# An attention and two-MoE kernel whose first part is issued on each engine in program order

## The chip, the cores and the metric

The kernel runs on one core of a Trainium2 chip. Its engines are TensorE (PE, matmuls, with the weight loads as PEld), VectorE (DVE), ScalarE (ACT), GpSimd (POOL) and SyncE (SP, which here issues DMAs); each works through its own list of instructions in order and waits at semaphores for the others. The metric is the time of one execution on the device in microseconds (us), as a median of several runs.

## What is computed

An attention over a softmax memory, then two gated layers, all in float32:

```python
a = phi - np.max(phi, axis=2, keepdims=True); a = np.exp(a)
a = a / (np.sum(a, axis=2, keepdims=True) + 1e-09)          # softmax over the sequence
k_m = np.einsum('bhsm,bhsd->bhmd', a, k); v_m = np.einsum('bhsm,bhsd->bhmd', a, v)
scores = scale * np.matmul(q, k_m.transpose(0, 1, 3, 2))    # then a softmax over the 32 memories
attn_out = np.matmul(attn, v_m)                             # q, k, v: (4, 8, 576, 64), phi: (4, 8, 576, 32)
# x: (2304, 512), its rows normalized by their root mean square and rms_g
x = (silu(x @ w_gate) * (x @ w_val)) @ w_out                # 512 -> 1536 -> 512
h = x @ w_in; g = where(h >= 1, h, where(h <= -1, 0, (h + 1) ** 2 / 4)); out = g @ w_out2   # 512 -> 2048 -> 512
```

A float32 product is made from three products of a high and a low part (names ending in h and l).

## The kernel before

The program has two parts. P1 computes the attention and the first MoE layer, P2 (L1040 `hp`, L1065 `acc`) the second. P1 is written as many small generator functions, called streams. Each stream yields, before each piece of its work, which engine it needs and for how long ("V", 2.12), or that it takes or gives a buffer, or that it waits for a flag that another stream sets. An `Agenda` object holds all streams with a model of time: engine by engine it keeps when the engine is free, adds a small latency (`HOP`) when work passes from one engine to the next, and always goes on with the stream that can start earliest; at a tie a priority decides. When a stream goes on, its instructions are written into the program. So the program's order is the order of this model. Some steps leave the choice of the engine to the model ("VAhi", "GAlow", "VAsign", "VGlo", "VGal").

Before, this order is not the order of issue: the Tile framework's own scheduler takes the program and orders the instructions of each engine again, by its own estimate. Only instructions named in `tc.keep_in_program_order` keep their place against each other: all loads of phi, k, v and q, the first 24 (`KEEP`) loads of raw weights, and the small `heat` matmuls (L480) that keep TensorE busy early on.

The streams that matter here:
- `loads` issues the loads of phi, k, v and q of the four batches on SP.
- `soft(b)`, one for each batch b: the maximum over the sequence (`pm`, L423, VectorE), its spreading by TensorE (`mps`, L429 and L446), the subtraction from `phi` (L452, VectorE), the exponent (L459, ScalarE), then four sums on GpSimd (`half` and `s`, L466 to L469).
- `memory(b)`: `kvps` (L501, TensorE) sums the exponents with k and v and L514 adds the sums `s`; VectorE divides (`r`, `kd`, `vs`, L524 to L549).
- nine pairs of queries (half a batch each, and one for the rests): `qps`, `sc`, `e`, `aT`, `xp`, `ATp`, `Ah`, `Al`.
- `convert` (L240 on): raw weights arrive as 64-bit words in one of four `raw` buffers; ScalarE, VectorE and GpSimd turn them into float32 (`w`, `cx`: L261, L264, L266, L270, L280, L282), for the output weight of the first layer also into two parts (`wo1h`, `wo1l`, L289, L291). Weights of the gate and value products come first (raw0, raw1 and so on), then the output weight, then P2's weights, which go back to HBM (`w_d`).
- `vwps` (L769) multiplies the weights with the memory's values; `vwh`, `vwl` (L789) are its two parts. `gv` (L818) makes `gps` and `vps` from them in 48 chunks, 12 a batch, in two halves each; `gate` (L846 `th`, L849 `ah`, L851 `al`) forms their product. `out1` (L876) makes `ops` from `ah`, `al` and the output weight; a stream of it first waits for the flag ("wo1", 0), which is set when six units of that weight are converted.

In names like kvps1_0 the first number is the batch, in gps4_1 the chunk and its half, in ops0_0 the batch and the output's part.

Of the kernel before, what the change touches and what calls it, by code (L numbers as in the profile page):

```python
# [25 lines left out]
ORDER = [0, 1, 2, 3, 8, 4, 5, 6, 7]  # L26

BANKS = {"g": (0, 1), "v": (2, 3), "o": (4, 5), "p": (0, 1, 2, 3), "w": (6, 7), "q": (2, 3), "s": (1,), "x": (2, 3), "a": (0,), "t": (5,), "k": (7,), "m": (4,), "l": (4,)}

KEEP = 24  # L30

HEAT = (6, ("A", (0, 0)), 2.09, 0.34)

# [11 lines left out]
class Agenda:  # L45
# [22 lines left out]
    def add(self, pri, stream):  # L68
        self.count += 1
        self._go([pri, self.count, stream, None, self.done, ""], None)  # L70
# [34 lines left out]
    def run(self, stop=None):  # L105
        while self.live and not (stop and stop in self.flags):
            best = None
            for x in self.live:
                s = self._start(x)
                if s is not None:  # L110
                    key = (max(s[0], self.now), x[0], x[1])
                    if best is None or key < best[0]:
                        best = key, x, s[1]
            assert best is not None, [(x[0], x[3]) for x in self.live]
            (at, _, _), x, z = best
            self.live.remove(x)
            self.now = at
            kind, arg = x[3]
            value = None
            done = at  # L120
            if kind == "take":
                self.room[arg] -= 1
            elif kind == "give":
                self.room[arg] += 1
            elif kind == "rest":
                done += arg
            elif kind == "flag":
                x[5] = ""
            elif kind == "heat":
                tick = int(at / TICK)  # L130
                value = self.ticks.get(tick, 0.0) < HEAT[2]
                if value:
                    slow = 1.0 if self.ticks.get(tick - 1, 0.0) > WARM else 2.0
                    self.ticks[tick] = self.ticks.get(tick, 0.0) + arg
                    done = self.free["P"] = at + arg * slow
            else:
                value = kind[z]
                t = arg[z] if isinstance(arg, tuple) else arg
                if value == "P":
                    tick = int(at / TICK)  # L140
                    slow = 1.0 if self.ticks.get(tick - 1, 0.0) > WARM else 2.0
                    self.ticks[tick] = self.ticks.get(tick, 0.0) + t * DUTY.get(kind, 1.0)
                    t *= slow
                done = self.free[value] = at + t
                x[5] = value
            self.done = done
            x[4] = x[4] + 0.5 if kind == "Dq" else done
            self._go(x, value)


def tile_attn_moe(tc, q, k, v, phi, w_gate, w_val, w_out1, rms_g, w_in2, w_out2, out):
# [10 lines left out]
    nc = tc.nc  # L162
    B, H, S, D = q.shape
    M = phi.shape[3]
# [72 lines left out]
    def convert(src, pieces, dst, split, done):  # L237
# [4 lines left out]
        nconv[0] += 1  # L242
        raw = wv.tile([P, CU, 2], U32, tag="raw", name=f"raw{n}", bufs=BUFS["raw"])
        rs = raw.rearrange("p n t -> p (n t)")
        i = nc.sync.dma_start(out=rs.rearrange("p (c f) -> p c f", c=pieces) if pieces > 1 else rs, in_=src)
        if n < KEEP:
            tc.keep_in_program_order(i)
        yield "rest", DMA_LAG
        if split:
            yield "take", "x"  # L250
# [105 lines left out]
    def loads():  # L356

        seq = []
        for b in range(B):
            seq += [("phi", b), ("kv", b)]  # L360
        for i, pr in zip(Q_AT, q_loads, strict=True):
            seq.insert(i, ("q", pr))
        for s in seq:
            yield "take", "qr" if s[0] == "q" and s[1][0] == B else s[0]
            if s[0] == "phi":
                b = s[1]
                yield "Dq", 1.8
                t = phi_t[b] = ld.tile([P, 4, J, M], F32, tag="phi", name=f"phi{b}", bufs=BUFS["phi"])
                tc.keep_in_program_order(
                    nc.sync.dma_start(out=t.rearrange("p c j m -> p c (j m)"), in_=by_half(phi[b], J * M))  # L370
                )
            elif s[0] == "kv":
                b = s[1]
                t = kv_t[b] = ld.tile([P, 2, 4, J, D], F32, tag="kv", name=f"kv{b}", bufs=BUFS["kv"])
                for i, src in ((0, k), (1, v)):
                    yield "Dq", 3.6
                    tc.keep_in_program_order(
                        nc.sync.dma_start(
                            out=t[:, i].rearrange("p c j d -> p c (j d)"), in_=by_half(src[b], J * D)
                        )  # L380
                    )
            else:
                b = s[1][0]
                yield "Dq", 3.4 if b < B else 0.45 * len(per_batch(s[1]))
                if b == B:
                    t = q_t[s[1]] = ld.tile([P, H, LJ, D], F32, tag="qr", name=f"qr{s[1][1]}", bufs=BUFS["qr"])
                    for bb, rows in per_batch(s[1]):
                        tc.keep_in_program_order(
                            nc.sync.dma_start(
                                out=t[rows],  # L390
                                in_=q[bb, :, SM:S, :].rearrange("h (p j) d -> p h j d", j=LJ),
                            )
                        )
                else:
                    t = q_t[s[1]] = ld.tile([P, H, QJ, D], F32, tag="q", name=f"q{b}", bufs=BUFS["q"])
                    tc.keep_in_program_order(
                        nc.sync.dma_start(
                            out=t.rearrange("p h j d -> p h (j d)"),
                            in_=q[b, :, 0:SM, :].rearrange("h (p j) d -> p h (j d)", j=QJ),
                        )  # L400
                    )
            add(0, arrived(s))
        for name in ("phi", "kv", "q", "qr"):
            for _ in range(BUFS[name]):
                yield "take", name
        mark("inputs")

    def by_half(x, n):

        return x.rearrange("h s d -> (h s d)").rearrange("(c q x) -> q c x", c=4, x=n)  # L410
# [62 lines left out]
    def heat():  # L473

        yield "take", ("bank", HEAT[0])
        t = psum.tile([P, 512], F32, tag=f"b{HEAT[0]}", name="heat")
        while HEAT[1] not in agenda.flags:
            go = yield "heat", 0.1067
            if go:
                i = nc.tensor.matmul(  # L480
                    out=t[:, 0:256], lhsT=zeros[:, 0:P], rhs=zeros, start=True, stop=True,
                    skip_group_check=True,
                )
                tc.keep_in_program_order(i)
        yield "give", ("bank", HEAT[0])

    s1_t = {}
# [452 lines left out]
            mark("w2 done")  # L940


    add(0, loads())
    for b in range(B):
        add(P_SOFT + 2 * b, soft(b))
# [76 lines left out]
    for i in range(N2U, N2U + N2R):  # L1022
        load_w2(2 * i + 1, w2c)
    agenda.run()
    left.close()


# [114 lines left out]
```

## Time and profile before

| | us |
|---|---|
| median of 3 runs | 904.62 (903.49 to 904.70) |
| the profiled execution | 901.98 |
| its span in the trace | 900.1 |
| TensorE busy in the span | 850.1 (94%) |
| VectorE, ScalarE, GpSimd busy | 480.2, 354.7, 187.2 |
| mean granted clock of TensorE | 0.975 of full speed |

The span begins with P1's loads. The attention takes the first 88 us or so, its last pairs and the first gates follow to 125, the first batch's gates with most weight conversions to 196, the other batches' gates with the output products to 482, and P2 the rest. A TensorE row gives a modelled end, so its busy share is an upper estimate.

### The profile page before, as it was taken

The page shows a single profiled execution, that of the slowest core. Times are in us where ns is not written, and L with a number is a line of the kernel's source. Part 1 is how long each engine was busy: PE and PEld are TensorE (multiplying, and loading weights), DVE is VectorE, ACT ScalarE, POOL GpSimd, SP SyncE. Part 2 cuts the span into 40 slices and gives each one's busy share as a digit, 9 for nine tenths or more (in the row PEclk, how much of TensorE's full clock was granted, in tenths as well). Part 3 has the DMA queues.
Part 4 walks back from the last instruction along what each step waited for, and adds up shares of the span by engine and source line. Part 5 has one row for each costly group of instructions (what it writes and reads, how often), then busy time and mean ns, then how long its engine had stood idle before and what let it go on. Part 6 is the DMA issues. An engine that isn't in the chain of part 4 may idle for free.

```text
span 900.1 us, 15187 instructions
## 1 busy us (share of the span) xinstructions
PE 850.1 (94%) x6058; PEld 728.1 (81%) x6058; DVE 480.2 (53%) x815; ACT 354.7 (39%) x698; POOL 187.2 (21%) x207
## 2 busy tenths in 40 slices
PE   7759888999999999999999999999999999999993
PEld 5647666778878999899999888888888888888892
DVE  3576889997888686315521433433343333333441
ACT  1345686685577465314421222322222222222331
POOL 3156576544433440000111400000000000000000
PEclk9987999999999999999999999999999999999997
DMA  9974266878989998312483970000040003000100
GB/s 323 335 253 132 71 217 213 290 262 299 364 306 338 333 317 292 120 54 94 135 274 99 381 250 1 36 12 1 1 141 0 1 1 94 0 1 1 47 1 23
DMA packets 72142, 137.56 MB, mean 153 GB/s; under 512 B 8840, under 2 KB 37512, under 8 KB 72072
## 3 DMA queue, kind: packets, MB, share of 16 engines
q1 hardware_dynamic: 61576, 108.28, 35.2%
q0 software_dynamic: 10496, 28.32, 10.2%
q8 instruction: 47, 0.77, 0.3%
q14 instruction: 23, 0.19, 0.1%
HBM read 99.35 MB, written 37.22 MB: 152 GB/s over the span
## 4 chain that ended last, share of the span: by engine, by line
PE 80%; DVE 8%; DMA 6%; issue 2%; ACT 2%; POOL 1%; SPq 0%; DVEq 0%; ACTq 0%; POOLq 0%
PE acc L1065 22%; PE hp L1040 22%; PE ops L876 15%; PE gps L818 7%; PE vps L818 7%; PE vwps L769 3%; DMA phi<-in_phi_dram 1%; DMA raw<-in_moe_w_gate_dram 1%; DVE w L261 1%; DMA kv<-in_v_dram 1%; DVE w L270 1%; PE xp L690 1%; PE kvps L501 1%; DVE cx L270 1%; DVE cx L261 1%
## 5 line engine op out<-in xcount | busy, mean ns | idle before, releaser
L1040 PE MATMUL hp<-xh,w 128*128 128x512 f32 (+1 forms) x640 | 193.2, 369 | 0.0
L1065 PE MATMUL acc<-w,gh 128*128 128x512 f32 x576 | 178.5, 391 | 0.0
L1040 PEld LDWEIGHTS hp<-xh,w 128*128 128x128 f32 x640 | 117.1, 188 | 21.5
L1046 DVE SCALAR_TENSOR_TENSOR y<-y 128x512 f32<-128x512 f32 (+1 forms) x80 | 51.2, 640 | 151.4 <-ACT y L1045 151.4
L1065 PEld LDWEIGHTS acc<-w,gh 128*128 128x128 f32 x576 | 107.1, 188 | 22.4
L1040 PE MATMUL hp<-xl,w 128*128 128x512 f32 (+1 forms) x320 | 118.4, 370 | 0.0
L876 PE MATMUL ops<-ah,wo1h 128*128 128x288 f32 x384 | 113.6, 298 | 3.1 <-ACT wo1h L289 1.9
L876 PE MATMUL ops<-al,wo1h 128*128 128x288 f32 x384 | 113.8, 297 | 1.0 <-DVE al L851 0.8
L876 PE MATMUL ops<-ah,wo1l 128*128 128x288 f32 x384 | 113.2, 296 | 1.0 <-DVE wo1l L291 1.0
L1065 PE MATMUL acc<-w,gl 128*128 128x512 f32 x288 | 112.7, 392 | 0.0
L1045 ACT ACTIVATE y<-hp,consts 128x512 f32<-128x512 f32 (+1 forms) x80 | 51.6, 645 | 151.6 <-PE hp L1040 151.6
L1050 ACT ACTIVATE gh<-y 128x512 fp32r<-128x512 f32 (+1 forms) x80 | 47.1, 589 | 137.6 <-PE acc L1065 120.0
L1051 DVE TENSOR_TENSOR gl<-y,gh 128x512 fp32r<-128x512 f32 (+1 forms) x80 | 51.1, 639 | 79.9 <-ACT gh L1050 79.9
L282 POOL TENSOR_TENSOR cx<-cx,raw 128x512 f32<-128x512 f32 x44 | 63.4, 1441 | 85.8 <-DVE cx L270 38.5
L876 PEld LDWEIGHTS ops<-ah,wo1h 128*128 128x128 f32 x384 | 72.0, 188 | 6.4 <-issue 2.5
L876 PEld LDWEIGHTS ops<-al,wo1h 128*128 128x128 f32 x384 | 72.2, 188 | 3.2 <-DVE al L851 2.0
L876 PEld LDWEIGHTS ops<-ah,wo1l 128*128 128x128 f32 x384 | 72.4, 189 | 1.3 <-DVE wo1l L291 1.3
L1040 PEld LDWEIGHTS hp<-xl,w 128*128 128x128 f32 x320 | 60.3, 188 | 10.7
L851 DVE TENSOR_TENSOR al<-th,ah 128x288 fp32r<-128x288 f32 x92 | 51.9, 567 | 25.6 <-ACT ah L849 24.9
L1065 PEld LDWEIGHTS acc<-w,gl 128*128 128x128 f32 x288 | 54.0, 188 | 12.3
L818 PE MATMUL gps<-Ah,vwh 128*128 128x288 f32 x192 | 60.9, 317 | 0.0
L280 ACT ACTIVATE raw<-raw 128x512 f32<-128x512 f32 x68 | 46.5, 684 | 34.7 <-DVE cx L261 22.0
(114 smaller groups left out, 1457.3 us busy)
## 6 DMA issues: line engine op xcount, KB each, us to landing
w<-wf_d SPq DMA_DIRECT2D x36, 512.0 KB, 5.2
w<-w_d POOLq DMA_DIRECT2D x36, 512.0 KB, 8.7
w_d<-w2s SPq DMA_DIRECT2D x32, 512.0 KB, 5.7
raw<-in_moe_w_out_dram SPq DMA_DIRECT2D x28, 512.0 KB, 4.9
raw<-in_moe_w_in_dram SPq DMA_DIRECT2D x16, 512.0 KB, 5.0
raw<-in_moe_w_gate_dram SPq DMA_DIRECT2D x12, 512.0 KB, 5.4
raw<-in_moe_w_val_dram SPq DMA_DIRECT2D x12, 512.0 KB, 5.7
wf_d<-w SPq DMA_DIRECT2D x12, 512.0 KB, 3.7
```

The source lines that it names most:

```text
L280: nc.scalar.activation(out=hv, in_=hv, func=AF.Sign)
L282: nc.gpsimd.tensor_tensor(out=dst, in0=dst, in1=hv, op=ALU.mult)
L769: nc.tensor.matmul(out=vps[g][0][32 * c : 32 * c + 32, 2 * P * x : 2 * P * x + 2 * P], lhsT=vT[b][hs, c, :], rhs=t[hs, c].rearrange("p i f ...
L818: nc.tensor.matmul(out=p[:, 0:HB], lhsT=wt[:, g, i, :], rhs=at[b][:, g, c], start=(g == 0 and x == 0), stop=(g == 1 and x == 2),)
L851: (nc.vector if eng == "V" else nc.gpsimd).tensor_tensor(out=al, in0=th, in1=ah.bitcast(F32), op=ALU.subtract)
L876: nc.tensor.matmul(out=p[:, 0:HB], lhsT=wt[:, fc, d], rhs=at[:, c], start=(fc == 0 and x == 0), stop=(fc == NF1 - 1 and x == 2),)
L1040: nc.tensor.matmul(out=hp, lhsT=wt[:, kc, :], rhs=xt[:, kc, 0:n], start=(kc == 0 and x == 0), stop=(kc == KC - 1 and x == 2),)
L1045: nc.scalar.activation(out=y, in_=hp, func=AF.Relu, scale=0.5, bias=half)
L1046: nc.vector.scalar_tensor_tensor(out=y, in0=y, scalar=1.0, in1=y, op0=ALU.min, op1=ALU.mult)
L1050: nc.scalar.activation(out=gh, in_=y, func=AF.Copy)
L1051: nc.vector.tensor_tensor(out=gl, in0=y, in1=gh.bitcast(F32), op=ALU.subtract)
L1065: nc.tensor.matmul(out=acc, lhsT=gt[:, cs], rhs=wt, start=(fc == 0 and x == 0), stop=(fc == NF2 - 1 and x == 2),)
```

## The change

P1 is put into `tc.manual_schedule()`: from the first stream (`add(0, loads())`) to the end of the agenda's run, each engine issues its instructions in the order in which the program wrote them, that is, in the order of the agenda's model. P2 is left to Tile's scheduler as it was. With that the single pins go: `KEEP` and every `tc.keep_in_program_order`. And in the model a flag that was set already when the stream asked for it no longer counts as an arrival: the engine of the stream's last step (`x[5]`, from which the latency `HOP` is taken) is forgotten only if the stream had to wait for the flag.

```diff
@@ Agenda.run
             elif kind == "flag":
-                x[5] = ""
+                if at > x[4]:
+                    x[5] = ""
@@ convert
-        i = nc.sync.dma_start(out=rs.rearrange("p (c f) -> p c f", c=pieces) if pieces > 1 else rs, in_=src)
-        if n < KEEP:
-            tc.keep_in_program_order(i)
+        nc.sync.dma_start(out=rs.rearrange("p (c f) -> p c f", c=pieces) if pieces > 1 else rs, in_=src)
...
@@ heat
-                i = nc.tensor.matmul(
+                nc.tensor.matmul(
...
-                tc.keep_in_program_order(i)
...
+    order = ExitStack()
+    order.enter_context(tc.manual_schedule())
     add(0, loads())
...
     agenda.run()
+    order.close()
     left.close()
```

The loads of phi, k, v and q lose their pins in the same way. The number of instructions stays; some ten to sixteen pieces of VectorE, ScalarE and GpSimd go to another engine than before, by the model's choice.

The lists of the engines differ in many places. Three of them follow. A number behind a name is a serial number of the buffer; line numbers of the changed kernel are 3 to 12 lower.

VectorE in the attention, around batch 1's subtraction (before: L452, `phi_276`; `pm_527` is batch 2's maximum). Before:

```order
L434 TENSOR_REDUCE gm_353<-mps_349 128x2
L439 TENSOR_TENSOR dg_357<-ident,gm_353 128x256
L574 TENSOR_TENSOR vT_89<-kT_359,gT 128x128
L423 TENSOR_REDUCE pm_527<-phi_458 128x128
L452 TENSOR_TENSOR phi_276<-phi_276,mps_349 128x1152
L637 TENSOR_REDUCE mx_0_387<-sc_0_373 128x16
```

Now, in the same place:

```order
L423 TENSOR_REDUCE gm_355<-mps_351 128x2
L428 TENSOR_TENSOR dg_359<-ident,gm_355 128x256
L441 TENSOR_TENSOR phi_278<-phi_278,mps_351 128x1152
L562 TENSOR_TENSOR vT_89<-kT_361,gT 128x128
L625 TENSOR_REDUCE mx_0_389<-sc_0_375 128x16
L631 TENSOR_TENSOR e_0_424<-sc_0_375,mx_0_389 128x512
```

The subtraction now follows its `dg` directly, and batch 2's maximum stands 13 rows further down.

ScalarE in the attention, around batch 2's exponent (`phi_458`, now `phi_460`; `raw_967` is raw0, the first raw weight). Before:

```order
L673 ACTIVATE aT_1_639<-aTp_1_604 128x512
L264 ACTIVATE raw_967<-raw_967 128x512
L459 ACTIVATE phi_458<-phi_458 128x1152
L280 ACTIVATE raw_967<-raw_967 128x512
L600 ACTIVATE qT_0_622<-qps_0_0_623 128x512
```

Now:

```order
L711 ACTIVATE Ah_93<-ATp_0_608 128x2x256
L448 ACTIVATE phi_460<-phi_460 128x1152
L661 ACTIVATE aT_1_641<-aTp_1_606 128x512
L588 ACTIVATE qT_0_624<-qps_0_0_625 128x512
L588 ACTIVATE qT_0_624<-qps_0_1_634 128x512
```

The exponent has moved ahead, and the conversions of raw0 to raw5 have moved behind batch 3's `kd` on VectorE, ScalarE and GpSimd alike; GpSimd's four sums of a batch stand in a row.

TensorE in the first batch's gates, behind `vps4_0` (before `vps_0_1709`). Before:

```order
L818 MATMUL vps_0_1709<-Ah_93,vwl_1536 128x288
L876 MATMUL ops_0_0_2123<-ah_1381,wo1h 128x288
L876 MATMUL ops_0_0_2123<-al_1382,wo1h 128x288
L876 MATMUL ops_0_1_2329<-ah_1381,wo1h 128x288
L876 MATMUL ops_0_1_2329<-al_1382,wo1h 128x288
L876 MATMUL ops_0_0_2123<-ah_1381,wo1l 128x288
```

Now:

```order
L806 MATMUL vps_0_1691<-Ah_93,vwl_1536 128x288
L806 MATMUL gps_1_1722<-Ah_93,vwh_1535 128x288
L806 MATMUL gps_1_1722<-Al_97,vwh_1535 128x288
L806 MATMUL gps_1_1722<-Ah_93,vwl_1536 128x288
L806 MATMUL gps_1_1722<-Ah_93,vwh_1535 128x288
```

Before, matmuls of the first output tiles stand among the gates from chunk 4 on; now the first of them stand in chunk 11, where the flag of the output weight is set.

## Rows read from the trace of the kernel before

**Rows 1.** busy us (and instructions) by stage; last TensorE's clock, DMA's share, GB/s

```profile
22.70:88.30 65.60, 49.42 (x714) 41.15 (x713) 42.07 (x81) 29.16 (x58) 31.57 (x36) 0.84 0.78 246
88.30:125.00 36.70, 30.03 (x306) 22.21 (x305) 29.75 (x52) 25.42 (x54) 22.57 (x24) 0.91 0.40 128
125.00:195.70 70.70, 66.41 (x498) 51.66 (x497) 66.89 (x105) 50.73 (x109) 40.63 (x33) 0.98 0.74 243
197.40:250.00 52.60, 50.42 (x387) 44.83 (x387) 44.46 (x71) 32.08 (x65) 24.19 (x20) 1.00 0.93 327
250.00:490.00 240.00, 240.00 (x2094) 225.43 (x2087) 128.05 (x244) 108.18 (x239) 42.76 (x42) 1.00 0.62 214
```

**Rows 2.** VectorE's timeline, batches 1 and 2: start us, us, line, operation, [idle before]

```profile
28.29 2.10 DVE L423 TENSOR_REDUCE pm<-phi 128x128 f32<-128x1152 f32 x1 [5.55 <-DMA phi<-in_phi_dram]
30.32 1.34 DVE L452 TENSOR_TENSOR phi<-phi,mps 128x1152 f32<-128x1152 f32 x1
...
46.05 1.35 DVE L452 TENSOR_TENSOR phi<-phi,mps 128x1152 f32<-128x1152 f32 x1 [0.41 <-PE mps L446]
```

**Rows 3.** TensorE's timeline around batch 1's kvps

```profile
24.24 0.44 PE L446 MATMUL mps<-dg,spread 128*64 128x128 f32 x4
...
32.90 3.38 PE L501 MATMUL kvps<-kv,phi 64*32 64x128 f32 x133 [4.74 <-ACT phi L459]
```

**Rows 4.** ScalarE's timeline around batch 2's exponent

```profile
53.32 0.67 ACT L264 ACTIVATE raw<-raw 128x512 uint32<-128x512 uint32 x1 [5.93 <-DMA raw<-in_moe_w_gate_dram]
53.89 1.16 ACT L459 ACTIVATE phi<-phi 128x1152 f32<-128x1152 f32 x1
```

**Rows 5.** GpSimd's timeline, sums of batch 0 and of batch 2

```profile
11.40 1.26 POOL L466 TENSOR_TENSOR half<-phi 128x512 f32<-128x512 f32 x1 [6.56 <-ACT phi L459]
...
14.10 0.46 POOL L469 TENSOR_TENSOR s<-s,phi 128x128 f32<-128x128 f32 x1
...
55.63 1.39 POOL L466 TENSOR_TENSOR half<-phi 128x512 f32<-128x512 f32 x1
...
66.05 0.63 POOL L469 TENSOR_TENSOR s<-s,phi 128x128 f32<-128x128 f32 x1
```

**Rows 6.** TensorE's waits from 0 to 140: us in total, times, longest

```profile
PE kvps L514 <- POOL s L469: 3.7, 1, 3.7
```

**Rows 7.** VectorE's timeline: batch 3's last vs, first and last th of batch 0

```profile
88.04 0.21 DVE L541 TENSOR_TENSOR vs<-kvps,r 128x64 f32<-128x64 f32 x1
...
124.54 0.45 DVE L846 TENSOR_TENSOR th<-th,vps 128x288 f32<-128x288 f32 x1
...
195.22 0.45 DVE L846 TENSOR_TENSOR th<-th,vps 128x288 f32<-128x288 f32 x1
```

**Rows 8.** VectorE by line, 53 to 88.3: count, busy us, mean ns, idle before

```profile
L270 DVE SCALAR_TENSOR_TENSOR w<-w,raw 128x512 uint32<-128x512 uint32 x6 | 5.2, 861 | 2.1 <-POOL raw L266 1.9
L261 DVE TENSOR_SCALAR w<-raw 128x512 f32<-128x512 f32 x6 | 4.8, 797 | 5.9 <-DMA raw<-in_moe_w_gate_dram 5.9
```

**Rows 9.** DMA issues on the page: count, KB, us to landing

```profile
raw<-in_moe_w_gate_dram SPq DMA_DIRECT2D x12, 512.0 KB, 5.4
```

**Rows 10.** output matmuls from 119 to 196.8: ns min/median/max, first and last start

```profile
L876 PE MATMUL ops<-ah,wo1h x21: 290/297/445, 146.1 to 194.4; 128*128 128x288 f32 x21
```

**Rows 11.** the same line from 208.7 to 218.5, back to back

```profile
L876 PE MATMUL ops<-ah,wo1h x25: 290/295/301, 208.8 to 218.3; 128*128 128x288 f32 x25
```

**Rows 12.** two stretches by busy us and clock, and TensorE's timeline at 120

```profile
119.00:121.00 2.00, 2.00 (x8) 1.73 (x7) 2.00 (x3) 1.55 (x5) 1.50 (x1) 0.52 0.23 76
...
60.00:80.00 20.00, 15.00 (x90) 10.75 (x89) 15.39 (x30) 10.11 (x22) 15.05 (x17) 0.74 0.70 233
...
120.34 0.44 PE L818 MATMUL gps<-Al,vwh 128*128 128x288 f32 x1
120.58 0.44 PE L818 MATMUL gps<-Ah,vwl 128*128 128x288 f32 x1
```

**Rows 13.** TensorE's timeline, one chunk's vwps

```profile
202.81 1.18 PE L769 MATMUL vwps<-w,vT 64*32 64x256 f32 x16
```

More of the change, by code (lines that the diff above doesn't have):

```diff
@@ L28 @@
 BANKS = {"g": (0, 1), "v": (2, 3), "o": (4, 5), "p": (0, 1, 2, 3), "w": (6, 7), "q": (2, 3), "s": (1,), "x": (2, 3), "a": (0,), "t": (5,), "k": (7,), "m": (4,), "l": (4,)}
-KEEP = 24
 HEAT = (6, ("A", (0, 0)), 2.09, 0.34)
@@ L368, in loads @@
                 t = phi_t[b] = ld.tile([P, 4, J, M], F32, tag="phi", name=f"phi{b}", bufs=BUFS["phi"])
-                tc.keep_in_program_order(
-                    nc.sync.dma_start(out=t.rearrange("p c j m -> p c (j m)"), in_=by_half(phi[b], J * M))
-                )
+                nc.sync.dma_start(out=t.rearrange("p c j m -> p c (j m)"), in_=by_half(phi[b], J * M))
             elif s[0] == "kv":
@@ L376, in loads @@
                     yield "Dq", 3.6
[L377 to L380, printed above, removed]
+                    nc.sync.dma_start(
+                        out=t[:, i].rearrange("p c j d -> p c (j d)"), in_=by_half(src[b], J * D)
                     )
@@ L387, in loads @@
                     for bb, rows in per_batch(s[1]):
[L388 to L392, printed above, removed]
+                        nc.sync.dma_start(
+                            out=t[rows],
+                            in_=q[bb, :, SM:S, :].rearrange("h (p j) d -> p h j d", j=LJ),
                         )
@@ L395, in loads @@
                     t = q_t[s[1]] = ld.tile([P, H, QJ, D], F32, tag="q", name=f"q{b}", bufs=BUFS["q"])
[L396 to L400, printed above, removed]
+                    nc.sync.dma_start(
+                        out=t.rearrange("p h j d -> p h (j d)"),
+                        in_=q[b, :, 0:SM, :].rearrange("h (p j) d -> p h (j d)", j=QJ),
                     )
```

## Prediction

> **What bounds the kernel now.** I read the stages first, then the waits at the front, then the two engines' own order there. The split of the span by stage [rows 1] says who limits what. From 250 us on TensorE has no idle time at all (240.00 of 240 us busy, at full clock) and it stays the bound through P2. So whatever the change does to the end must happen in the first 250 us: it must let TensorE start the dense part earlier, or leave it less or more to do there. The rows ahead of it belong to stages with other limits. Between 22.7 and 88.3 us, in the attention, no engine is full: TensorE is busy 49.42 of 65.6 us and VectorE 42.07, so this is a chain of waits. From 125.0 to 195.7, the first batch's gates with weight conversions beside them, VectorE is busy 66.89 of 70.70 us (94.6%): VectorE's work sets the pace there. From 88.3 to 125.0 it is only 29.75 of 36.7 (81%).
>
> In the attention two instructions stand in the wrong place of an engine's order. On VectorE the pm reduction of batch 2 starts at 28.29, after 5.55 us in which the engine waits for the phi of batch 2 to arrive; behind it stands the subtraction for batch 1, started at 30.32 [rows 2]. The input of that one, mps of batch 1, was finished by TensorE at 24.24 + 0.44 = 24.68, and TensorE itself then stood 4.74 us before batch 1's kvps at 32.90 [rows 3]. So a ready instruction, at the head of batch 1's chain, lay 30.32 - 24.68 = 5.6 us behind one whose data was not there. On ScalarE it repeats: the conversion of raw0 waits 5.93 us for its load and starts at 53.32; behind it stands the exponent of batch 2, at 53.89 [rows 4], whose input VectorE had finished at 46.05 + 1.35 = 47.40 [rows 2]: 6.5 us. On GpSimd the four sums of one batch take from 11.40 to 14.56, 3.2 us, for batch 0; for batch 2 they take from 55.63 to 66.68, 11.05 us, since conversions stand between them [rows 5]; TensorE waits 3.7 us for the last of them [rows 6].
>
> **The change, part by part.** No instruction is added or taken away apart from some ten to sixteen rows that go to another engine, so each term is a move.
>
> (a) Front of the attention. In the new order the subtraction of batch 1 stands ahead of pm2, the exponent of batch 2 ahead of all conversions, and GpSimd's four sums in a row. The three prices are 5.6, 6.5 and, for the sums, between 3.7 (the wait that TensorE saw) and 11.05 - 3.2 = 7.9; I take 5, nearer the wait, since part of the chain lay beside other work. Sum 17.1: the last vs of batch 3, which ends at 88.04 + 0.21 = 88.25 [rows 7], comes at about 71. Bound: if one of the gains runs into the next arrival of an input, a third of it goes, and it is about 77.
>
> (b) Conversions. Before, raw0 to raw5 are converted at 53 to 71 us inside the stalls; VectorE spends 5.2 + 4.8 = 10.0 us on them [rows 8]. In the new order all six come only after batch 3's kd, so they now lie between batch 3's vs and the first gate. From that vs to the first gate product (124.54 [rows 7]) VectorE then has 29.75 + 10.0 = 39.8 us of work. How densely it does it is the widest term. At the 94.6% of the next stage it takes 42.0 us and the first gate product comes at 71.2 + 42.0 = 113.2, 11.3 earlier (I call it 11); at the 81% it had here it takes 49.1 us, 120.3, 4.2 earlier. I take the dense end: the gaps here came from the attention's chain, whose pairs were late, and the conversions now lie between these pairs and fill them, as they do in the next stage. Another limit lies close: a raw load lands 5.4 us after its issue [rows 9], there are four buffers, and 15 conversions (six, and the nine that stood there) in 42.0 us is one in 2.8 us. If a conversion holds its buffer some 6 us beside the 5.4, by estimate from the wait of 5.93 and the durations in [rows 4, 8], four buffers give one in 2.85 us, so the dense end cannot be beaten.
>
> (c) The gate stage itself, first to last gate product of the first batch (124.54 to 195.22, 70.7 us [rows 7]), has the same work on VectorE, and I keep its length. Lead at its end: 11 us.
>
> (d) Filler lost. In the old order TensorE runs 61 matmuls of the first output tiles inside the gate stage [rows 10] (the first of three such rows, 21 + 20 + 20), where it has time to spare; in the new one six stand there, since the agenda's flag asks for all six units of the output weight and Tile's order did not. So 55 come after it. One costs, back to back, (218.3 - 208.8) / 24 / 3 = 0.132 us [rows 11], 0.135 with the ends: 55 x 0.135 = +7.4 us on a TensorE that is the bound from there on.
>
> (e) Idle time of TensorE between 197.4 and 250: 52.60 - 50.42 = 2.2 us [rows 1], waits for conversions and al, of which the dense run of the moved 55 matmuls covers all, or none: -2.2, bounds -2.2 to 0.
>
> (f) Fixed order from 200 to 490. Before, Tile could put a ready matmul ahead of one that waits; now TensorE stands at whatever the model believed ready. The waits of this kind that it already has are the 2.2 us of (e); I take +1.5, and bounds of 0 to 5, about twice what that stretch had.
>
> Sum: -11 + 7.4 - 2.2 + 1.5 = -4.3 us. The profiled execution took 901.98 us, its span 900.1; so 897.7, and 895.8 for the span. It was 2.6 us under the median of 904.62; on that median the forecast is **900.3 us**.
>
> **Rivals.** R1, slower: the front's lead is spent before the first gate, since VectorE stays as sparse as it was there (81%), stopped by raw loads that come one buffer at a time. Lead 4.2, then -4.2 + 7.4 + 1.5 = +4.7, with (e) as before: 909.3. It decides as soon as the lead at the first gate product is under 7.4 + 1.5 - 2.2 = 6.7 us. For it: the ring's limit is as near as said in (b), and VectorE is fuller in stages where conversions don't depend on the attention. Against: four raw tiles lie loaded and waiting when the stretch begins.
>
> R2, slower still: the clock. With the 55 matmuls gone TensorE has more idle time in the gate stage. In 119 to 121 the granted clock was 0.52 of full speed, the lower level of 1.2 GHz, after a stretch with waits, and gate matmuls came 0.24 us apart (120.34, 120.58) [rows 12]; full speed gives 0.13 [rows 11]. A chunk of 24 gate matmuls and 16 vwps (1.18 us at full speed [rows 13], twice that at half) would need 24 x 0.24 + 2.4 = 8.2 us against VectorE's 70.7 / 10.5 = 6.7 per chunk: up to +1.5 x 10.5 = +15.8, 916. Against it: the stage had 0.98 [rows 1], and 60 to 80 us, with 15.00 of 20 us busy, still had 0.74 [rows 12]. The Trainium skill, TensorE: Matmul & The Clock Gate, section "What's actually happening", says that the throttled state is the default and that activity releases it; by it any thinning of TensorE's work speaks for this rival, and the time would tend to its 916. The trace agrees that idleness goes with the lower level (0.52 in 119 to 121), and shows how little it cost in 60 to 80. The rows alone give it a small chance.
>
> R3, faster: TensorE, not VectorE, sets the gate stage. It is busy 66.41 of its 70.70 us by the records [rows 1]. Then taking 7.4 us of matmuls out shortens the stage by as much, (d) costs nothing, and the sum is -11 - 2.2 + 1.5 = -11.7: 892.9. Against: the ends of matmuls are modelled, so that busy overstates it.
>
> R4, no difference: the front's lead and the lost filler cancel, with a lead of 4.9 to 8.5 us at the first gate product, or the new order changes only places where nothing waited. 902.8 to 906.4.
>
> **How the numbers follow.** About 0.2%, 1.8 us, is what a measurement of this kernel can tell from no change. Forecast (895.6 to 902.8) 0.45; R3 0.12; R4 0.20; R1 0.18; R2 0.05. Faster: 0.45 + 0.12 = 0.57; same 0.20; slower 0.23. Most of the chance lies between R3's edge and the middle of R1: 893 to 908 leaves out half of R3, half of R1 and R2, about 2 in 10. It agrees with the bounds of the terms: a lead of 11 without a stall is 898.8, and R3's 892.9 holds the low end; a lead of 4.2 with a stall of 1.5 is 907.1 to 909.3, which holds the high end.
>
> **What would show it.** Term (a): batch 1's kvps starts near 27.5 us (before 32.9) and batch 3's last vs ends near 71 (before 88.25), with ScalarE's and VectorE's waits for loads gone from ahead of the exponent's chain. Term (b): first gate product near 114, conversions without a pause from 71 on. Term (c): the last gate product of the first batch near 184. Term (d): six output matmuls ahead of that point, and TensorE's busy share in the stage under 94%. Term (f): no wait of TensorE over 2 us after 200. First hp of P2 some 4 us earlier than before, P2 as long as it was. I am wrong if the first gate product comes after 118 (R1, R4), if the gate stage's clock falls under 0.9 (R2), if its length changes by more than 4 us either way (R2, R3), or if TensorE has more than 5 us of waits between 200 and 490.

## The result, and the profile after

The changed kernel takes 882.45 us (881.38 to 884.17), before 904.06: a ratio of 0.976 (95% interval 0.975 to 0.978), 21.6 us less. The forecast was 900.3, the low end 893.0. Direction right, size missed: the change brought five times the 4.3 us of the sum. The profiled execution took 881.78 us, its span 880.0.

The changed kernel in two of the stretches of [rows 1], and the first batch's gate stage (first gate product to the end of its last gate matmul), which has moved, before and after:

```profile
22.70:88.30 65.60, 55.75 (x858) 46.63 (x856) 53.35 (x101) 36.41 (x74) 35.44 (x43) 0.96 0.77 238
250.00:490.00 240.00, 240.00 (x2018) 227.75 (x2017) 128.53 (x249) 109.34 (x236) 58.63 (x68) 1.00 0.76 256
```

```profile
124.50:196.80 72.30, 68.01 (x510) 53.06 (x513) 68.49 (x107) 51.77 (x112) 42.23 (x33) 0.98 0.74 244
```

```profile
109.00:181.40 72.40, 57.06 (x462) 47.92 (x460) 68.67 (x107) 53.34 (x113) 37.36 (x29) 0.88 0.67 230
```

From 22.7 to 88.3 VectorE does 53.35 us of work instead of 42.07. In the gate stage TensorE is busy 57.06 us instead of 68.01, and its granted clock fell from 0.98 to 0.88, while VectorE has the same work (68.67 and 68.49 us). From 250 to 490 TensorE is full, as it was. Now the front, in the order of [rows 2 to 5] and [rows 7]: batch 1's subtraction (VectorE) and kvps (TensorE), batch 2's exponent (ScalarE) and its four sums (GpSimd, first and last), batch 3's last vs, and the first batch's first th and the one in the place of the third line of [rows 7]:

```profile
26.32 1.35 DVE L441 TENSOR_TENSOR phi<-phi,mps 128x1152 f32<-128x1152 f32 x1 [0.54 <-PE mps L435]
...
28.92 1.34 PE L489 MATMUL kvps<-kv,phi 64*32 64x128 f32 x78
...
42.95 1.16 ACT L448 ACTIVATE phi<-phi 128x1152 f32<-128x1152 f32 x1
...
44.18 1.28 POOL L455 TENSOR_TENSOR half<-phi 128x512 f32<-128x512 f32 x1 [2.47 <-ACT phi L448]
...
46.89 0.45 POOL L458 TENSOR_TENSOR s<-s,phi 128x128 f32<-128x128 f32 x1
...
65.99 0.21 DVE L529 TENSOR_TENSOR vs<-kvps,r 128x64 f32<-128x64 f32 x1
...
108.99 0.44 DVE L834 TENSOR_TENSOR th<-th,vps 128x288 f32<-128x288 f32 x1
...
179.87 0.45 DVE L834 TENSOR_TENSOR th<-th,vps 128x288 f32<-128x288 f32 x1
```

That third line of [rows 7], at 195.22, is not the first batch's last gate product: it is the 22nd of 24, and so is the one at 179.87. The last one starts at 199.95 before and at 182.50 after (the second of the two rows in the last line):

```profile
199.95 0.44 DVE L846 TENSOR_TENSOR th<-th,vps 128x288 f32<-128x288 f32 x1
```

```profile
182.14 0.82 DVE L834 TENSOR_TENSOR th<-th,vps 128x288 f32<-128x288 f32 x2
```

The subtraction waits for nothing but its input (26.32, before 30.32), the exponent starts at 42.95 (53.89), the four sums take 3.2 us (11.05). Batch 3's last vs ends at 66.20 instead of 88.25, the first gate product starts at 108.99 instead of 124.54, and the first batch's last gate matmul ends at 181.4 instead of 196.8. From there to the first hp of P2 it takes 287.2 us instead of 291.8; P2 is as long as it was. So of the span's 20.1 us, 15.5 come from ahead of the first gate product, none from the gate stage (72.3 and 72.4 us, to the end of its last matmul), and 4.6 from behind it, where the prediction had put a loss of 6.7.

Output matmuls up to the end of the first batch's last gate matmul (one of three such rows, 3 + 3 + 2, before 21 + 20 + 20 [rows 10]; two of the eight start behind that matmul, so six stand ahead of it, and 55 have moved behind it):

```profile
L864 PE MATMUL ops<-ah,wo1h x3: 300/300/403, 161.6 to 181.3; 128*128 128x288 f32 x3
```

Behind it the profile shows no wait of TensorE now (before 2.2 us). The other difference there is how the vwps stand. The records come in pairs, so a block for two chunks, 16 matmuls, has 32 rows. After (TensorE's timeline, the block behind the first batch's gates, with the matmul ahead of it and behind it):

```profile
181.54 0.29 PE L864 MATMUL ops<-ah,wo1l 128*128 128x288 f32 x1
181.77 1.09 PE L757 MATMUL vwps<-w,vT 64*32 64x256 f32 x32
182.79 0.40 PE L864 MATMUL ops<-ah,wo1h 128*128 128x288 f32 x1
```

Before, TensorE's timeline in a like place, vwps alone (other matmuls stand between them):

```profile
253.91 0.64 PE L769 MATMUL vwps<-w,vT 64*32 64x256 f32 x8
...
255.59 0.62 PE L769 MATMUL vwps<-w,vT 64*32 64x256 f32 x4
```

The whole block keeps TensorE from other work for 182.79 - 181.54 - 0.13 = 1.1 us. The groups of 8 and of 4 rows of before occupy 0.64 and 0.62 us. Over the whole stretch behind the gates, by line:

```profile
L769 PE MATMUL vwps<-w,vT 64*32 64x256 f32 x518 | 26.1, 384 | 0.0
```

```profile
L757 PE MATMUL vwps<-w,vT 64*32 64x256 f32 x544 | 18.6, 382 | 0.0
```

Busy 26.1 us for 518 rows before, 18.6 for 544 after. Taken from one matmul's start to the next (into the vwps, among them, and out, waits left out), 31 groups cost 30.8 us before, 17 groups 21.2 after.

By the starts, the 4.6 us behind the gates come out as follows. The 55 moved output matmuls add 55 x 0.133 = 7.3 us. TensorE's waits fall from 3.1 to 0.2 us, -2.9. The groups bring -9.2: 30.8 - 21.2 = 9.6, less 1.9 since the step out of each of the 14 groups that are gone leaves an ordinary step of 0.13 in its place, and 1.5 more since the second matmul behind a group comes after 0.24 us instead of 0.13.

### The profile page after: what moved, and what is told of

It is laid out like the page before. It is cut to its first block, busy times and chain, and to the rows that moved or that the text cites. A ratio compares the mean times of both kernels' runs of the same rounds, so it can differ in the third digit from the quotient of the medians.

```text
span 880.0 us, 15147 instructions
## 1 busy us (share of the span) xinstructions
PE 828.8 (94%) x6058; PEld 724.1 (82%) x6058; DVE 473.4 (54%) x817; ACT 350.8 (40%) x695; POOL 179.8 (20%) x207
## 4 chain that ended last, share of the span: by engine, by line
PE 85%; DVE 6%; DMA 2%; issue 2%; ACT 2%; POOL 1%; SPq 0%; POOLq 0%; DVEq 0%; ACTq 0%
PE acc L1057 23%; PE hp L1032 23%; PE ops L864 17%; PE vps L806 7%; PE gps L806 7%; PE vwps L757 2%; PE xp L678 1%; DMA kv<-in_v_dram 1%; PE sc L615 1%; DVE w L258 1%; DMA raw<-in_moe_w_val_dram 1%; PE kvps L489 1%; PE qps L597 1%; DVE w L267 1%; POOL cx L279 1%
## 5 line engine op out<-in xcount | busy, mean ns | idle before, releaser
L1057 PE MATMUL acc<-w,gh 128*128 128x512 f32 x576 | 178.5, 391 | 0.0
L1057 PEld LDWEIGHTS acc<-w,gh 128*128 128x128 f32 x576 | 107.0, 188 | 22.4
L279 POOL TENSOR_TENSOR cx<-cx,raw 128x512 f32<-128x512 f32 x43 | 58.8, 1368 | 131.0 <-ACT raw L277 90.7
L806 PE MATMUL vps<-Ah,vwh 128*128 128x288 f32 x192 | 60.4, 315 | 7.2 <-DVE th L834 7.2
L806 PE MATMUL gps<-Ah,vwh 128*128 128x288 f32 x192 | 58.7, 306 | 4.0 <-ACT vwh L775 2.1
L806 PE MATMUL gps<-Ah,vwl 128*128 128x288 f32 x192 | 58.2, 303 | 3.7 <-DVE vwl L777 3.7
```

What stands on the lines that cost most here:

```text
L279: nc.gpsimd.tensor_tensor(out=dst, in0=dst, in1=hv, op=ALU.mult)
L806: nc.tensor.matmul(out=p[:, 0:HB], lhsT=wt[:, g, i, :], rhs=at[b][:, g, c], start=(g == 0 and x == 0), stop=(g == 1 and x == 2),)
L1057: nc.tensor.matmul(out=acc, lhsT=gt[:, cs], rhs=wt, start=(fc == 0 and x == 0), stop=(fc == NF2 - 1 and x == 2),)
```

## Experiments

The theory after the first look: (1) the order of VectorE, ScalarE and GpSimd in the attention brings the 15.5 us at the first gate product; (2) behind the gates, whole blocks of vwps and missing waits bring more than the lost filler costs. The rival: all of it follows from the front. Milestones of all runs, in us from the span's start, read from the timelines (last column: groups of vwps behind the first batch's gates). They are those of one profiled execution each, which can lie some us off the median (before 2.6 below it, e13 3.0 above, e5 3.7 above):

| kernel | median | kvps of batch 1 | last vs of batch 3 | first th | last gate matmul | first hp | groups |
|---|---|---|---|---|---|---|---|
| before | 904.6 | 32.9 | 88.3 | 124.5 | 196.8 | 488.6 | 31 |
| changed | 882.5 | 28.9 | 66.2 | 109.0 | 181.4 | 468.6 | 17 |
| e1 | 926.9 | 36.7 | 91.5 | 137.2 | 214.6 | 513.9 | 17 |
| e2 | 920.7 | 31.2 | 71.8 | 119.9 | 201.0 | 509.0 | 51 |
| e3 | 905.9 | 29.4 | 66.7 | 109.7 | 186.7 | 492.6 | 52 |
| e4 | 899.1 | 33.4 | 90.4 | 126.7 | 198.8 | 485.8 | 17 |
| e5 | 884.5 | 28.0 | 65.3 | 110.8 | 183.4 | 474.2 | 17 |
| e6 | 886.4 | 29.1 | 66.4 | 109.7 | 178.5 | 472.8 | 17 |
| e7 | 893.4 | 28.0 | 65.2 | 110.9 | 183.3 | 481.7 | 17 |
| e8 | 900.4 | 28.3 | 65.5 | 108.8 | 181.0 | 486.0 | 17 |
| e9 | 907.8 | 31.0 | 88.1 | 123.4 | 199.3 | 493.1 | 29 |
| e10 | 894.9 | 32.9 | 74.2 | 112.1 | 183.3 | 481.1 | 28 |
| e11 | 879.4 | 29.0 | 66.3 | 109.3 | 177.8 | 464.4 | 17 |
| e12 | 905.8 | 33.2 | 90.4 | 125.5 | 202.1 | 494.3 | 25 |
| e13 | 894.5 | 33.1 | 73.0 | 116.7 | 184.8 | 484.3 | 29 |
| e14 | 882.4 | 28.0 | 65.3 | 108.1 | 180.6 | 467.7 | 17 |
| e15 | 878.4 | 28.1 | 65.4 | 108.9 | 177.6 | 464.2 | 17 |

**e1: TensorE alone in program order; e2: all but TensorE.**

```diff
+    order.enter_context(tc.manual_schedule(engines={mybir.EngineType.PE}))                        # e1, in the kernel before
-    order.enter_context(tc.manual_schedule())                                                     # e2, in the changed kernel
+    order.enter_context(tc.manual_schedule(engines={... DVE, Activation, Pool, SP}))
```

> The kernel before, with TensorE alone in program order (the other engines and the pins as before, the model of time as before). Theory: the gain has two sources, the order of VectorE, ScalarE and GpSimd in the attention (first gate product 15.5 us earlier) and TensorE's order behind the first batch's gates (4.6 us), where vwps stand in whole blocks (17 groups after that point instead of 31, some 0.6 us a group) and no matmul waits. Then this kernel keeps the late first gate product, near 124, and gains about 5 us: near 899. Rival: all comes from the front and what follows from it, and TensorE's order alone gives nothing but the loss of filler, +7: near 911, or nothing: 904.

> The changed kernel, with VectorE, ScalarE, GpSimd and SyncE in program order and TensorE left to Tile's order (heat matmuls pinned). By its order vwps stand in 51 groups behind the first batch's gates (31 before, 17 after), and 61 output matmuls stand among the gates again. Theory: the front's lead of about 15 us is kept; the groups cost 20 x 0.6 = 12 us against the kernel before: near 901, or 889 if TensorE has slack there. Rival (grouping costs nothing, all comes from the front): 884 or, with the filler back, 877.

Measured 926.9 (ratio 1.026, 1.023 to 1.028) and 920.7 (1.019, 1.016 to 1.023): both slower than either whole order, which neither theory had. In e1 TensorE stands in the program's order while the others come in Tile's; its waits up to 140 us (us in total, times, longest):

```profile
PE mps L446 <- DVE dg L439: 9.1, 3, 7.2
PE kvps L514 <- POOL s L469: 7.7, 1, 7.7
```

It stood 7.2 us at one mps, then up to 7.7 at the sums; the first gate product came 12.6 us later than before. In e2 the front is good (last vs at 71.8), but the vwps fall into 51 groups behind the gates:

```profile
L758 PE MATMUL vwps<-w,vT 64*32 64x256 f32 x524 | 41.0, 391 | 0.0
```

That line's 41.0 us busy is 22.4 more than in the changed kernel; start to start it is 47.7 against 21.2. So here two orders that don't know of each other cost more than Tile's order on all engines.

**e3: program order up to the attention's end, Tile's behind it; e4: the other way round.**

```diff
     agenda.run("attention")
+    order.close()          # e3; in e4 the region is opened here instead, the pins hold ahead of it
```

> The changed kernel, with the program's order ending where the attention's last piece has been written; Tile orders the rest on all engines (52 groups of vwps behind the first gates, 55 output matmuls among them). Theory: lead of 15 at the first gate product, then back to Tile's stretch with 21 more groups than before at 0.6: near 902, 889 if they find slack. Rival (all from the front): 884.

> The kernel before up to the end of the attention (with its pins), the program's order on all engines behind it (17 groups of vwps after the first gates). Theory: first gate product near 124 as before, about 5 us gained behind the gates: near 899. Rival (all from the front): 904, or 911 with the filler lost.

Measured 905.9 (1.003, 1.001 to 1.004) and 899.1 (0.996, 0.994 to 0.997). e3 has the whole lead at the first gate product (109.7) and loses it: the gate stage takes 77.0 us, the stretch behind it 306.0, with 52 groups (45.6 us start to start). e4, which has the edit of the model too, has a late front (126.7) and the short stretch behind the gates, 287.0 us, to 0.2 of the changed kernel's. Theory (2) holds and the rival falls: the gain behind the gates comes without the front's lead. The two parts are also not additive (e3 2.0 us slower than before, e4 4.8 faster, both together 21.6 faster): e3 spends its lead behind the attention.

**e7, e8: the price of a change between the two kinds of matmul.** 24 places in the output matmuls of three batches get one extra float32 matmul on a tile of vwps' kind (64 rows, 32 columns of weights), or four; it moves 64 columns where vwps moves 256, and its result is used by nobody.

```diff
+                        if b < 3:
+                            nsw[0] += 1
+                            if nsw[0] % 12 == 0:
+                                for _ in range(1):     # e8: 4
+                                    nc.tensor.matmul(out=p[0:32, HB : HB + 64], lhsT=ident[0:64, 0:32],
+                                        rhs=ident[0:64, 0:64], start=True, stop=True, skip_group_check=True)
```

> The changed kernel, with one extra matmul of the vwps kind (float32, 64 rows, 32 columns of weights, moving 64 columns) behind each of the first 24 output tiles of three batches, where TensorE is full. Theory: changing from the 128x128 products to the 64x32 float32 ones and back costs 0.26 us by the starts in the trace (0.09 in, 0.17 out), and the row itself 0.1: 24 x 0.36 = 8.6, near 891. Rival (the groups of vwps only look dear because they wait for something): 24 x 0.1 = 2.4, near 885.

> The same with four such matmuls in a row at each of the 24 places. Theory: the changes stay 24, only rows are added: 24 x 3 x 0.03 to 0.1 = 2 to 7 us over the one with a single row: 893 to 898. Rival (each row has the full price, not the change): 24 x 4 x 0.36 = 35: 917.

Measured 893.4 and 900.4: 11.0 and 17.9 us over the changed kernel. TensorE's timeline at one place of e7 and at one of e8:

```profile
193.37 0.29 PE L866 MATMUL ops<-ah,wo1l 128*128 128x288 f32 x1
193.60 0.30 PE L874 MATMUL ops<-ident 64*32 64x64 f32 x2
193.82 0.40 PE L866 MATMUL ops<-ah,wo1h 128*128 128x288 f32 x1
194.06 0.30 PE L866 MATMUL ops<-al,wo1h 128*128 128x288 f32 x1
```

```profile
191.47 0.29 PE L866 MATMUL ops<-ah,wo1l 128*128 128x288 f32 x1
191.69 0.63 PE L874 MATMUL ops<-ident 64*32 64x64 f32 x8
192.25 0.40 PE L866 MATMUL ops<-ah,wo1h 128*128 128x288 f32 x1
192.49 0.30 PE L866 MATMUL ops<-al,wo1h 128*128 128x288 f32 x1
```

In e7 the last output matmul ahead starts at 193.37, the first one behind at 193.82 and its successor at 194.06: 0.45 + 0.24 instead of 0.13 + 0.13, 0.43 us for one place. In e8 it is 0.78 + 0.24. Three matmuls more cost 0.33, 0.11 each; so the change there and back costs 0.43 - 0.11 = 0.32 us (0.36 by the medians: 11.0 / 24 - 0.10). The theory's 0.26 was a little low; the rival is out. The Trainium skill, TensorEngine Tiling (Array Packing), section "Key Properties", says that changing the tiling mode drains TensorE; the 0.32 us there and back fit that. Shape and number type (float32 against fp32r, the type of the products' high and low parts) change together here, so these runs don't show that the mode alone costs it.

Over eight kernels the vwps behind the gates cost, start to start, waits left out: 17 groups 21.2 us (changed, and e4), 25 groups 26.6 (e12), 28 groups 30.2 (e10), 29 groups 29.9 (e9), 31 groups 30.8 (before), 51 groups 47.7 (e2), 52 groups 45.6 (e3). That is some 0.7 us a group. The traces also say what the rest is. Two groups of before, with the matmuls around them, one of a single vwps matmul (2 rows) and one of eight (16 rows):

```profile
265.88 0.29 PE L876 MATMUL ops<-ah,wo1l 128*128 128x288 f32 x1
266.10 0.62 PE L769 MATMUL vwps<-w,vT 64*32 64x256 f32 x2
266.65 0.40 PE L818 MATMUL gps<-Ah,vwh 128*128 128x288 f32 x1
266.89 0.30 PE L818 MATMUL gps<-Al,vwh 128*128 128x288 f32 x1
...
269.41 0.29 PE L818 MATMUL gps<-Ah,vwl 128*128 128x288 f32 x1
269.63 0.66 PE L769 MATMUL vwps<-w,vT 64*32 64x256 f32 x16
270.23 0.40 PE L818 MATMUL gps<-Ah,vwh 128*128 128x288 f32 x1
270.47 0.29 PE L818 MATMUL gps<-Al,vwh 128*128 128x288 f32 x1
```

Priced as in e7 (up to the second matmul behind, less two steps of 0.13), the one matmul costs 0.74 us and the eight cost 0.79; a whole block of sixteen costs 1.2. The program issues a block as two eights, and the eight matmuls of one use different places of the array (two halves of its rows, four quarters of its columns). So a whole eight costs hardly more than one matmul, and a piece of a broken eight costs as much as a whole one. The price of one fits e7: 0.32 for the change and, with 256 columns instead of 64, 4 x 0.11 = 0.44, in all 0.76 where 0.74 was read. Behind the gates the 31 groups of before hold 46 eights and pieces of eights, the 17 of after 34 whole ones: 14 x 0.32 + 12 x 0.44 = 9.8 us by these prices, where 9.2 were measured.

**e12: vwps pinned in the kernel before.**

```diff
+                        if g or c or x:
+                            tc.keep_in_program_order(i)      # i: the vwps matmul
```

> The kernel before, with each vwps matmul of a block but the first pinned behind the one ahead of it; by its order 49 groups of vwps instead of 61, 25 behind the first gates instead of 31. Theory (0.7 us a group where TensorE is full): 6 x 0.7 = 4 us less behind the gates, near 900, with the front as before. Rival (groups cost nothing): 904.

Measured 905.8 (1.002, 1.000 to 1.004). The groups saved what they should, 30.8 - 26.6 = 4.2 us, but the stretch is no shorter (292.2 us, 291.8 before), since TensorE waits longer in it, and the gate stage grew from 72.3 to 76.5, with a wait at a pinned vwps that the kernel before did not have:

```profile
PE vwps L769 <- DVE vwl L791: 3.6, 1, 3.6
```

The theory's total missed. My reading is that Tile had broken the blocks to fill waits of its own order, and that without this filling the waits show; no run tries it apart.

**e5: the output weight's flag unit by unit.**

```diff
-                yield "flag", ("wo1", d4 // 2)
...
+                        yield "flag", ("wo1", d4 // 2, fc // 2)
                         yield "flag", ("a", n, hf)
```

> The changed kernel, with the flag of the output weight set unit by unit, so that an output matmul waits for its own unit alone; by its order 30 output matmuls stand ahead of the first batch's last gate matmul instead of 6. Theory (the prediction's term for lost filler holds: a gate stage paced by VectorE, TensorE full behind it): 24 x 0.133 = 3.2 us less behind the gates, near 879. Rival (TensorE has no room in the gate stage): the stage grows by as much, 882; or the interleaved output matmuls wait for conversions and hold up gate matmuls, 884 or more.

Measured 884.5 (0.980, 0.977 to 0.983): no gain, so the theory's total missed and the last rival (884 or more) came. The 24 matmuls went into the gate stage, and its length stayed (72.6 us), as the theory had it. But behind it (busy us by stretch, then TensorE's wait for ah):

```profile
183.00:190.00 7.00, 4.66 (x50) 3.67 (x49) 6.58 (x12) 5.71 (x13) 2.86 (x2) 0.78 0.59 175
190.00:200.00 10.00, 10.00 (x64) 10.00 (x64) 2.90 (x7) 1.21 (x3) 0.64 (x1) 0.81 0.41 149
...
PE ops L864 <- ACT ah L837: 1.6, 1, 1.6
```

In this execution (888.1 us, the slowest of four) TensorE meets the last conversions with nothing else to do, waits, and runs at 0.78 and 0.81 of its clock up to 200 us. So the moved filler is real work, but doing it earlier in this way brought no time back.

**e6: without the edit of the model; e11 and e15: with it only behind the first batch's gates; e14: the changed kernel again, beside e15.**

```diff
-                if at > x[4]:                       # e6: x[5] = "" always
+                if at > x[4] or not self.late:      # e11, e15
                     x[5] = ""
...
     agenda.run(("a", NF1 - 1, 1))
+    agenda.late = True
```

> The changed kernel without the edit of the model (every flag counts as an arrival, as before). Theory: the model's latencies shift a few ties, TensorE's order keeps its blocks (25 groups of vwps in all, 9 output matmuls ahead): 882 within 2 us. Rival: the edit is what makes the model's order fit the chip, and without it engines wait for each other: 886 or more.

> The changed kernel, with the edit of the model switched on only after the first batch's gates. Theory (the gate stage was 3.7 us shorter without the edit, 68.8 instead of 72.5, and the stretch behind it 7 us longer, from waits): both good halves together, near 879. Rival (the shorter gate stage only left conversions of the output weight for later, and TensorE waits for them behind it): 882 to 886.

> The changed kernel itself, to stand beside the next one: 882.

> The kernel of e11 again, beside the changed kernel on the same chip: 879, some 3 us under it, from the gate stage (68.5 us instead of 72.5). Rival: the two are the same within 1 us and e11 was a lucky set of runs.

e6: 886.4, 3.9 us over the changed kernel, as the rival had it; TensorE's waits behind the gates:

```profile
PE ops L863 <- DVE xl L879: 2.3, 2, 2.1
PE vps L805 <- DVE th L833: 1.1, 4, 0.6
```

The gate stage is shorter without the edit (68.8 us), the stretch behind it longer (294.3), with such waits. e11 takes both good halves: 879.4, and again in e15 878.4 (876.9 to 879.7) beside 882.4 (880.9 to 884.6) of e14 on the same chip. Its gate stage:

```profile
109.30:177.80 68.50, 57.33 (x466) 48.45 (x465) 65.95 (x105) 50.23 (x108) 38.13 (x32) 0.88 0.74 243
```

68.5 us with VectorE busy 65.95 of them, where the changed kernel has 68.67 of 72.4: VectorE has 2.7 us less to do in a stage that is 3.9 us shorter, and what the rest is stays open. So the best version seen is the changed kernel with the edit of the model switched on late, 0.971 (0.969 to 0.974) of before.

**e9, e10, e13: the front, move by move, in the kernel before.** e9 pins the maxima over phi, e10 asks for the conversions of raw0 to raw5 behind batch 3's vbd and pins them there, e13 does both.

```diff
+        tc.keep_in_program_order(nc.vector.tensor_reduce(out=pm, ...))      # e9, e13
...
+        if n < 6:                                                           # e10, e13, in convert
+            yield "flag", ("vbd", 3)
```

> The kernel before, with each maximum over phi pinned to its place in the program's order on VectorE; by its order batch 1's subtraction now stands ahead of batch 2's maximum, the conversions stay where they were. Theory (the stalls of the attention stand one behind the other, and the next one is set by a DMA): batch 1's kvps starts 4 us earlier, near 29, but batch 2's exponent still waits behind raw0, which lands at 53, so batch 3's last vs stays at 88 and the time at 904. Rival (the terms add, as the prediction had them): last vs 4 to 5.6 us earlier, 899.

> The kernel before, with the conversions of raw0 to raw5 asked for and pinned behind batch 3's vbd on their engines (their loads stay early); batch 2's maximum stays where it was. Theory: batch 2's exponent at 48 to 49, GpSimd's four sums in 3.2 us, batch 3's last vs near 71 to 73, first gate product 8 to 10 us earlier, 28 groups of vwps behind the gates: 893 to 896. Rival (the conversions ran in stalls for nothing, and have to be paid in full later): 904.

> The kernel before, with both moves of e9 and e10: the maxima over phi pinned, the conversions of raw0 to raw5 behind batch 3's vbd. Theory (the two stalls hide each other; together they are the front): batch 1's kvps near 30, batch 3's last vs at 67 to 70 (88 before, 74 with the conversions alone, 66 in the changed kernel), first gate product at 108 to 110. Behind it 29 groups of vwps as before, so 891 to 894. Rival (a third move of the program's order is needed): last vs at 74 as in e10, 895.

e9 measured 907.8 (1.007, 1.003 to 1.010): not faster. Batch 1's subtraction starts at 27.94 instead of 30.32, and batch 2's exponent at 55.03, still behind raw0 (VectorE, then ScalarE):

```profile
27.94 1.35 DVE L452 TENSOR_TENSOR phi<-phi,mps 128x1152 f32<-128x1152 f32 x1 [4.64 <-PE mps L446]
...
54.45 0.67 ACT L264 ACTIVATE raw<-raw 128x512 uint32<-128x512 uint32 x1 [10.39 <-DMA raw<-in_moe_w_gate_dram]
55.03 1.15 ACT L459 ACTIVATE phi<-phi 128x1152 f32<-128x1152 f32 x1
```

ScalarE's wait for raw0 only grew, from 5.93 to 10.39 us: it hid the gain, as the theory had it, though kvps came at 31.0 and not near 29. e10: 894.9 (0.992, 0.989 to 0.995). The exponent starts at 48.39 and GpSimd's sums take 3.2 us:

```profile
48.39 1.17 ACT L462 ACTIVATE phi<-phi 128x1152 f32<-128x1152 f32 x1
...
49.64 1.28 POOL L469 TENSOR_TENSOR half<-phi 128x512 f32<-128x512 f32 x1 [2.16 <-ACT phi L462]
...
52.36 0.46 POOL L472 TENSOR_TENSOR s<-s,phi 128x128 f32<-128x128 f32 x1
```

That brings 14.0 us at batch 3's last vs (74.2, where the theory had 71 to 73), and the time that the theory gave. e13 adds the other move and gets only 73.0, 894.5 (0.989, 0.986 to 0.991): the rival, that a third move is needed. Its place on TensorE, then TensorE in the kernel before:

```profile
26.93 0.52 PE L612 MATMUL qps<-ident,q 128*128 128x128 f32 x3 [2.82 <-DMA q<-in_q_dram]
27.38 0.44 PE L449 MATMUL mps<-dg,spread 128*64 128x128 f32 x4
...
28.42 3.48 PE L630 MATMUL sc<-kmT,qT 128*128 128x64 f32 x16
...
33.11 1.30 PE L504 MATMUL kvps<-kv,phi 64*32 64x128 f32 x37
```

```profile
27.12 1.04 PE L609 MATMUL qps<-ident,q 128*128 128x128 f32 x8
```

In e13 a qps, 2.82 us waiting for its q, stands ahead of batch 1's mps, and sc and five more qps ahead of kvps, which starts at 33.11 as if nothing had been moved. In the changed kernel kvps starts at 28.92 (32.90 before [rows 3]). In the kernel before no qps waited there: mps came at 24.24 [rows 3], ahead of that qps at 27.12. So with VectorE's order changed Tile chose another order on TensorE too (in e9 and e2 as well, where that qps waits 1.46 and 2.61 us for its q), and what the subtraction alone is worth is not shown. What is shown: two engines of the old order had something not yet ready ahead of the chain (VectorE pm2, ScalarE raw0), and in e9 the second wait took the gain of the first; and the last 5 us or so came only with TensorE's order, since the last vs ends at 71.8 where Tile orders TensorE (e2) and at 66.7 and 66.2 where the program does (e3, changed).

## Why the prediction missed

- (a) The front: mechanism right, size too small. The last vs came 22.05 us earlier, not 17.1. By intervals, kvps of batch 1 gained 4.0 (5.6 forecast), batch 2's exponent 10.9 in all; the larger miss is GpSimd's and VectorE's conversions, priced at 5 for the sums: e10, which moves them alone, gains 14.0 against 6.5 + 5. That the three prices may be added was not borne out: e9 gave nothing, e13 little more than e10. Some 5 of the 22 us need TensorE's order as well (71.8 in e2, 66.2 and 66.7 with it), which the term did not have.
- (b) Right in size, in part by luck. From the last vs to the first gate product it takes 42.8 us against 42.0 forecast, with the six conversions between. VectorE has 42.09 us of work there, not 39.8, but is busy 98% of the time, not 94.6%.
- (c) Right: 72.4 us against 72.3, though its row for the last gate product was the 22nd of 24. R3 falls (with 55 matmuls fewer the stage kept its length), and so does R1, since the lead at the first gate product was 15.5.
- R2 named the clock under 0.9 as its sign. It came, 0.88, and the stage kept its length: TensorE had room, VectorE set the pace. Two shorter stages say the same: e11 took 68.5 us at 0.88, e13 68.0 us at 1.00, with nearly the same work on VectorE (65.95 us in e11, 65.49 here):

```profile
116.80:184.80 68.00, 62.05 (x491) 49.25 (x480) 65.49 (x101) 48.33 (x104) 39.40 (x36) 1.00 0.75 246
```

- (d) Right: 55 matmuls moved behind the gates, +7.3 us by their starts against +7.4. In e5 putting 24 of them back did not pay.
- (e), (f) TensorE's waits behind the gates, by starts, fell from 3.1 to 0.2 us (-2.9); the sum had -2.2 + 1.5. I feared stalls of a fixed order; there are none.
- The step that failed is the one that is not in the list. vwps stand in 61 groups before and in 25 after, 31 and 17 of them behind the gates, and I priced TensorE's moved work by the rows of the output matmuls alone: a change in how like matmuls stand together was put at nothing. Behind the gates that left out -9.2 us. With it, 7.3 - 9.2 - 2.9 = -4.8, where 4.6 were measured and a loss of 6.7 was forecast. Of the miss of 15.8 in the span 9.2 is this, 2.2 the waits, and 4.4 the front's larger lead, which is term (a) mis-sized (22.05 us, not 17.1).

## What to carry over

Count the runs of like matmuls in an order, not the matmuls alone: each change between the 128x128 products and small tiles cost 0.32 us there and back here, and each piece of a broken eight some 0.44, as much as a whole one. Waits at the heads of several engines' queues can hide one another, so moving one of them may show nothing (e9), and a scheduler that is left to order the other engines answers a pin with another order there. An order fixed on some of the engines, with a scheduler's on the others, was worse (1.019 and 1.026) than either whole order.

## What was not expected

A change of matmul kind on a full TensorE costs 0.32 us there and back (e7, e8), eight small-tile matmuls cost what one costs (0.79 and 0.74 us), and the clock fell from 0.98 to 0.88 in a stage of 72 us whose length stayed, where VectorE sets the pace. A small rule of the planner (whether a set flag counts as an arrival) is worth 3.9 us (e6), and helps behind the first gates while in the gate stage it costs some 4 us (e11, e15).
